# A planner that counts TensorE's instruction pages, and MLP products mixed into the attention from the seventh chunk

## The chip, the cores and the metric

One core of one Trainium2 chip runs the kernel. The metric is device time in microseconds (us) of one launch; lower is better. All times of before are of the same program on the same inputs.

## The reference

Inputs: `q`, `k`, `v` of shape (4 batches, 8 heads, 768 tokens, 64), and an MLP's weights. First a retention layer, then a gated MLP on its output:

```python
gamma = 1.0 - 2.0 ** (-5.0 - np.arange(H))
for t in range(S):
    state = gamma * state + einsum('bhd,bhe->bhde', k[:, :, t], v[:, :, t])
    y[:, :, t] = scale * einsum('bhd,bhde->bhe', q[:, :, t], state)
x = y.transpose(0, 2, 1, 3).reshape(B, S, H * D)           # (4, 768, 512)
gate_pre = sum(conv_w[k] * xp[:, k:k + S, :] for k in range(5))   # xp: x with 4 zero rows ahead
gate = 1 / (1 + exp(-gate_pre))
out = (gate * (x @ w_val)) @ w_out
```

The weights come as 64-bit numbers and are turned into float32 on the chip. The two large products are done as three products each (high by high, high by low, low by high part).

## The kernel before, in words

**Attention.** The 768 tokens of 4 batches are cut into 24 chunks of 128 tokens, numbered g = 0 to 23; chunk g is batch g mod 4 of row g // 4. A chunk is 1 MB of `q`, `k`, `v`, `k` (tile `att`, five buffers, `LB`). GpSimd scales its `v` (`decay`, L236). TensorE computes `scores` (L246), VectorE masks them into `u` (`mask`, L256), then TensorE runs `block_a` (products of `u` with `v`, L284, and the first half of the state, L268) and `block_b` (second half of the state, L268, and the products of the two state snapshots with `q`, L284). ScalarE takes the snapshots (`snap`, L279), VectorE writes the result to `x` (`evac`, L329). All these products are of 64x64 tiles. One such float32 matmul appears twice in the trace: `scores` is 32 matmuls there, a chunk with both halves of the state 128.

**MLP.** It works on a row of four chunks (512 columns of `x`), in 4 tiles m of 128 channels. `split` makes the high and low parts of `x` (L338 on ScalarE, L342 on GpSimd). `conv` is five taps into a PSUM tile `acc`: the first on ScalarE, four on VectorE (L432, "taps" below), of which the planner may give two to TensorE (`pe_tap`, L441). A sigmoid follows (L448). `val_tile` is 12 matmuls of 128x512 (L458), `gated` multiplies by the gate on VectorE (L467), and ScalarE and GpSimd split the result (L474, L478). `out_tile` is 12 matmuls (L486), a copy and a store. There are 24 tiles of each kind, 576 matmuls.

**Weights.** Eight weight tiles `wst` of 512 KB (four buffers) are converted (`convert`): five VectorE instructions (L375, L381, L387, L391, L404), a ScalarE and a GpSimd step in between (L396, L400), then the split (L415, L419). L404 waits for GpSimd's L400.

**PSUM.** The first `EARLY` chunks use two banks of scores in turn (`sy`, and `sy1`, which prints as `sy_97`). From chunk `EARLY` on only `sy` is used; the place of `sy1` goes to the MLP's `mm` tiles, and `block_b` of a chunk ends with the `scores` of the next one.

**The order.** Every step is declared with a due time, an engine, a cost, and what it reads and writes. `plan` (L50) sorts the steps by due time, then runs a list scheduler over them: an engine takes, among its steps that are ready by the declared costs, the one of earliest due time. The order that results is each engine's program; the due times and the costs themselves do nothing on the chip. Each engine runs its instructions strictly in that order and waits where an input is late. The first MLP product may come only after the last user of `sy1`:

```python
if n == m == i == 0:
    steps[-1].after = [
        s for s in steps if any(isinstance(k, Slot) and k.ring in ("s1", "y1") for k in s.reads + s.writes)
    ]
```

Of the kernel before, what the change touches and what calls it, by code (L numbers as in the profile page):

```python
# [18 lines left out]
NPAIR = 4  # L19
TAPS = 5  # L20
WARM = 13
EARLY = 10
LB = 5
XB = 4
XS = 6
GV = 6
LATENCY, LANDING = 0.15, 1.8
TINY = 2.0 ** -15 * (1.0 + 1.0 / 8.0)
LO, HI = slice(0, HALF), slice(HALF, P)

# [8 lines left out]
class Step:  # L39
    def __init__(self, due, engine, cost, reads, writes, fn, args):  # L40
        self.due, self.engine, self.cost, self.fn, self.args = due, engine, cost, fn, args
        self.reads, self.writes = reads, writes
        self.waits, self.then = set(), []
        self.next = []
        self.after = []
        self.ready = 0.0
        self.other = None


def plan(steps):  # L50

    steps = sorted(steps, key=lambda s: s.due)
    writer, readers, rings, users = {}, {}, {}, {}
    for i, s in enumerate(steps):
        s.index = i
        for k in s.writes:
            if isinstance(k, Slot) and k not in users:
                users[k] = []
                rings.setdefault(k.ring, []).append((k, s))
        for k in s.reads + s.writes:  # L60
            if isinstance(k, Slot):
                users[k].append(s)

    def wait(s, b):
        if b is not s and s not in b.then:
            s.waits.add(b.index)
            b.then.append(s)

    for s in steps:
        for k in s.reads + s.writes:  # L70
            if k in writer:
                wait(s, writer[k])
        for k in s.writes:
            for b in readers.pop(k, []):
                wait(s, b)
        for k in s.reads:
            readers.setdefault(k, []).append(s)
        for k in s.writes:
            writer[k] = s
        for b in s.after:  # L80
            wait(s, b)
    for ring in rings.values():
        for i, (k, s) in enumerate(ring):
            if i >= k.bufs:
                for b in users[ring[i - k.bufs][0]]:
                    wait(s, b)
            if i and s not in ring[i - 1][1].next:
                s.waits.add(ring[i - 1][1].index)
                ring[i - 1][1].next.append(s)
    clock, free = {}, {}  # L90

    def offer(s):
        free.setdefault(s.engine, []).append(s)
        if s.other:
            free.setdefault(s.other[0], []).append(s)

    for s in steps:
        clock.setdefault(s.engine, 0.0)
        if not s.waits:
            offer(s)  # L100
    order = []
    while any(free.values()):
        start, _, e = min(
            (max(clock[e], min(s.ready for s in f)), e, e) for e, f in free.items() if f
        )
        s = min((s for s in free[e] if s.ready <= start), key=lambda s: (s.engine != e, s.index))
        free[s.engine].remove(s)
        if s.other:
            free[s.other[0]].remove(s)
            if s.engine != e:  # L110
                s.engine, s.cost, s.fn = s.other
        order.append(s)
        clock[e] = start + s.cost
        for t in s.next:
            t.ready = max(t.ready, start)
            if t not in s.then:
                t.waits.discard(s.index)
                if not t.waits:
                    offer(t)
        for t in s.then:  # L120
            late = LANDING if e == "DMA" else 0.0 if t.engine == e else LATENCY
            t.ready = max(t.ready, clock[e] + late)
            t.waits.discard(s.index)
            if not t.waits:
                offer(t)
    assert len(order) == len(steps)
    return order
# [3 lines left out]
def tile_retention_gated_mlp(  # L131
# [215 lines left out]
    raws = {}  # L347

    def load_w(n):
        st = stage.tile([P, 512, 2], I32, name="wst", bufs=4)  # L350
        nc.sync.dma_start(
            out=st,
            in_=w64[n // 4, n % 4].bitcast(I32).rearrange("p (n two) -> p n two", two=2),
        )
        raws[n] = st

    cvt = {}
# [166 lines left out]
    LATE_AT = 28.7  # L524
    LATE_STEP = 3.05
    MLP_AT = 31.2
    MLP_STEP = 12.8
    SPLIT_LEAD = 5.4
    CONV_LEAD = 6.1
    W_AT = (14.4, 15.6, 15.6, 22.7, 32.7, 35.7, 38.7, 41.7)  # L530

    def load_at(due, g):
        a = [("att", g % LB, "qk"), ("att", g % LB, "vk")]
        if g == 0:
            at(due, "DMA", 1.4, [], a[0:1], load, g, slice(0, 2))
            at(due, "DMA", 0.2, [], ["small"], get, small_sb, small)
            at(due, "DMA", 1.4, [], a[1:2], load, g, slice(2, 4))
            at(due, "DMA", 0.1, [], ["cwraw"], get, cw_raw,
               conv_w.bitcast(I32).rearrange("p (n two) -> p n two", two=2))
            at(due, "DMA", 0.1, [], ["pos"], get, pos_sb, pos)  # L540
        else:
            at(due, "DMA", 2.6, [], a, load, g)
# [14 lines left out]
    def attention(g, t, ahead):  # L557
# [6 lines left out]
        sc = scored[g]  # L564
        y = Slot("y%d" % bank, 1)
        slow = 1.3 if g < 8 else 1.0
        at(t - 3.0, "POOL", 1.05, ["small"], [vk], decay, g)
        if not (g and ahead_of(g - 1)):
            at(t, "PE", 0.6 * slow, [qk, "sy%d" % bank], [sc], scores, g)
            if bank in summed:  # L570
                steps[-1].after.append(summed[bank])
        u = Slot("u", 2)
        at(t + 0.7, "DVE", 0.7, [sc, "small"], [u], mask, g)
        taken = [Slot("snap", 3) for _ in range(2)]
        z = ("z", b)
        if c > 0:
# [1 line left out]
        else:  # L578
            taken = taken[1:]
        at(t + 1.5, "PE", 1.05 * slow, [u, vk], [y, z], block_a, g)  # L580
        at(t + 2.7, "ACT", 0.38, [z], taken[-1:], snap, g, 1)
        more, new = [], []
        if ahead and g + 1 < NG:
            scored[g + 1] = Slot("s%d" % bank, 1)
            more, new = [("att", (g + 1) % LB, "qk")], [scored[g + 1]]
        at(t + 3.3, "PE", (1.5 if ahead else 0.9) * slow, [qk, vk] + taken + more, [y, z] + new,
           block_b, g, ahead)
        summed[bank] = steps[-1]
        if b == 0:
            xbufs[c] = Slot("x", XB)  # L590
            last = [xbufs[c - 1]] + [("x", c - 1, i) for i in range(B)] if c else []
            at(t + 3.5, "ACT" if c else "DVE", 0.25, last,
               [xbufs[c]] + [("x", c, i) for i in range(B)], new_x, c)
        at(t + 5.0, "DVE", 0.7, [y, ("dec", c % 2), xbufs[c]], [("x", c, b)], evac, g)
        if g + LB < NG:
            load_at(t + 3.4, g + LB)
        if c + 1 < NCH:
# [5 lines left out]
    def convert(t, n):  # L603
        raw = wsts[n] if n != "cw" else "cwraw"
        acc, top, rest = Slot("acc", 2), Slot("top", 2), Slot("rest", 2)
        k = 0.25 if n == "cw" else 1.0
        for i, (engine, cost, fn, reads, writes) in enumerate((
            ("DVE", 0.7, cv_bits, [raw], [acc, top, rest]),
            ("DVE", 0.7, cv_top, [raw, acc], [top]),
            ("DVE", 0.7, cv_exp, [top], [acc]),  # L610
            ("DVE", 0.7, cv_rest, [raw, acc], [rest]),
            ("ACT", 0.67, cv_size, [raw], [acc]),
            ("POOL", 1.1, cv_sum, [top], [rest]),
            ("DVE", 0.7, cv_flush, [acc], [rest] if n != "cw" else [rest, "cw"]),
        )):
            at(t + 0.01 * i, engine, cost * k, reads, writes, fn, n)
        if n != "cw":
            at(t + 0.08, "ACT", 0.62, [rest], [("wh", n)], cv_round, n)
            at(t + 0.09, "POOL", 1.3, [rest, ("wh", n)], [("wl", n)], cv_low, n)

    wsts = [Slot("wst", 4) for _ in range(2 * NPAIR)]

    def load_w_at(t, n):
        at(t, "DMA", 1.3, [], [wsts[n]], load_w, n)
# [1 line left out]
    def conv(n, m, t):  # L626
# [1 line left out]
        x = [xbufs[n]] + [("x", n, b) for b in range(B)]  # L628
        at(t, "ACT", 0.7, x + ["cw"], [acc], tap, n, m, 0)
        for k in range(1, TAPS):  # L630
            at(t + 0.1 * k, "DVE", 0.76, x + ["cw", ("diag", m)], [acc], tap, n, m, k)
            if k <= 2:
                steps[-1].other = ("PE", 1.05, pe_tap)
        gates[n, m] = Slot("gate", 2)
# [10 lines left out]
    def val_tile(n, m, t):  # L645
        bank = Slot("mm", 2)
        gate_of = gates[n, m]
        for i in range(3 * NPAIR):
            part = i // NPAIR
            reads = [("wl" if part == 1 else "wh", m)]  # L650
            reads.append(parts[n, i % NPAIR][part == 2])
            at(t + MM * i, "PE", MM, reads, [bank], val, n, m, i)
            if n == m == i == 0:
                steps[-1].after = [
                    s for s in steps if any(isinstance(k, Slot) and k.ring in ("s1", "y1") for k in s.reads + s.writes)
                ]
        gv, gl = gparts[n, m] = Slot("gvh", GV), Slot("gvl", GV)
        at(t + 3.0, "DVE", 0.7, [bank], [gate_of], gated, n, m)
        at(t + 3.1, "ACT", 0.62, [gate_of], [gv], round_gv, n, m)
        at(t + 3.2, "POOL", 1.3, [gate_of, gv], [gl], rest_gv, n, m)  # L660

    def out_tile(n, b, t, cols=1):
        width = DM // cols
        for q in range(cols):
# [3 lines left out]
            for i in range(3 * NPAIR):  # L668
                ct = i // 3
                reads = [gparts[n, ct][i % 3 == 2], ("wl" if i % 3 == 1 else "wh", 4 + ct)]  # L670
                at(t0 + i * MM / cols, "PE", MM / cols, reads, [bank], outp, n, b, i, cs)
            o = Slot("o", 2)
            at(t0 + 12 * MM / cols + 0.1, "ACT", 0.6 / cols, [bank], [o], store, n, b, cs)
            at(t0 + 12 * MM / cols + 0.2, "DMA", 0.1, [o], [], send, n, b, cs)
# [3 lines left out]
    at(0, "ACT", 1.5, [], ["table"], first_sigmoid)  # L678
    load_at(0, 0)
    for due, w, n in ((0.1, 1, 0), (0.2, 0, 1), (0.3, 1, 1), (0.4, 0, 2), (0.5, 1, 2), (0.6, 0, 3), (0.7, 1, 3), (0.8, 0, 4)):  # L680
        (load_w_at if w else load_at)(due, n)
        if due == 0.3:
            at(due, "DMA", 0.2, [], ["eye"], get, eye_sb, eye)
    at(5.05, "PE", 1.0, ["pos", ("att", 0, "vk")], ["sy1"], first_pos)
# [120 lines left out]
```

## Time and profile before

| | us |
|---|---|
| three timed runs | 237.19, 239.09, 240.62; median 239.09 |
| the profiled execution, its own time | 237.6 |
| its span, first to last instruction | 235.8 |
| TensorE busy | 210.0 (89% of the span) |
| VectorE busy | 140.0 (59%) |
| ScalarE, GpSimd busy | 105.4, 105.7 (45% each) |
| mean granted TensorE clock | 0.957 |

The time is the span and 1.8 us around it. Three views matter: the busy time of each engine by stretch, with the granted clock (1.00 is 2.4 GHz, 0.50 is 1.2 GHz); the chain that ended last, which is followed back from the last instruction and names at each step what it waited for ("issue" is a wait for nothing that the profile shows); and the instructions of one engine in order of time.

### The profile page before, as it was taken

What the parts mean: (1) busy time and instruction counts of PE and PEld (TensorE: products, weight loads), DVE (VectorE), ACT (ScalarE), POOL (GpSimd) and SP (SyncE); (2) the same over time, 40 slices, a digit from 0 to 9 for tenths busy, and PEclk for the clock granted to TensorE, in tenths of its full rate; (3) what the DMA queues carried; (4) which work ended last, traced back from release to release, by engine and by line L of the source; (5) the groups of instructions that cost most, each with busy time, mean ns of one, the idle gap of its engine ahead of it and who ended that gap; (6) DMA issues with size and microseconds to landing.
All of it is one profiled execution on the core that took longest, in us unless ns stands there. A gap on an engine that the chain in (4) does not pass through costs nothing.

```text
span 235.8 us, 7969 instructions
## 1 busy us (share of the span) xinstructions
PE 210.0 (89%) x3553; PEld 165.6 (70%) x3553; DVE 140.0 (59%) x211; ACT 105.4 (45%) x218; POOL 105.7 (45%) x93
## 2 busy tenths in 40 slices
PE   8356675767989999999999999999999999999994
PEld 3255574556667777776767788887888888888884
DVE  0575655957878899897435973349816961831100
ACT  2371337427445766650256233664366426520312
POOL 0274549764984996131138112492168208220400
PEclk9977559979999999999999999999999999999999
DMA  5999949997835665655010111111111111111122
GB/s 169 384 425 417 403 140 383 327 327 267 327 113 197 226 199 200 210 231 211 10 40 3 47 47 46 46 46 44 47 44 44 44 44 47 57 64 56 44 92 89
DMA packets 8822, 36.32 MB, mean 154 GB/s; under 512 B 1106, under 2 KB 1618, under 8 KB 5844
## 3 DMA queue, kind: packets, MB, share of 16 engines
q1 hardware_dynamic: 8788, 35.82, 40.7%
q8 instruction: 28, 0.46, 0.8%
q14 instruction: 6, 0.05, 0.1%
HBM read 29.52 MB, written 6.29 MB: 152 GB/s over the span
## 4 chain that ended last, share of the span: by engine, by line
PE 83%; issue 7%; DMA 6%; DVE 1%; ACT 1%; SPq 0%; ACTq 0%
PE mm L458 30%; PE mm L486 29%; PE sy L284 11%; DMA att<-in_att_dram 6%; PE sy L246 6%; PE z_ps L268 6%; PE acc L441 1%; DVE x L329 1%; DVE u L256 1%; ACT snap L279 0%; ACT dec L317 0%; ACT acc L430 0%; ACT o_sb L496 0%; SPq L224 0%; ACTq L496 0%
## 5 line engine op out<-in xcount | busy, mean ns | idle before, releaser
L432 DVE SCALAR_TENSOR_TENSOR acc<-x,cw_sb,acc 128x512 f32<-128x512 f32 x93 | 69.4, 753 | 21.1 <-ACT acc L430 18.9
L478 POOL TENSOR_TENSOR gvl<-gate,gvh 128x512 fp32r<-128x512 f32 x24 | 30.9, 1297 | 38.9 <-ACT gvh L474 29.3
L342 POOL TENSOR_TENSOR xl<-x,xh 128x512 fp32r<-128x512 f32 x24 | 30.5, 1291 | 30.7 <-PE mm L458 30.7
L236 POOL TENSOR_TENSOR att<-att,small_sb 128x512 f32<-128x512 f32 x24 | 25.0, 1044 | 32.2 <-DMA att<-in_att_dram 23.8
L486 PE MATMUL mm<-woh,gvl 128*128 128x512 f32 (+1 forms) x100 | 39.0, 390 | 0.0
L486 PE MATMUL mm<-wol,gvh 128*128 128x512 f32 (+1 forms) x100 | 39.0, 390 | 0.0
L486 PE MATMUL mm<-woh,gvh 128*128 128x512 f32 (+1 forms) x100 | 38.9, 389 | 0.0
L496 ACT COPY o_sb<-mm 128x512 f32<-128x512 f32 (+1 forms) x25 | 14.3, 571 | 37.3 <-PE mm L486 37.3
L279 ACT COPY snap<-z_ps 128x256 f32<-128x256 f32 x44 | 15.0, 374 | 33.4 <-PE z_ps L268 31.8
L467 DVE TENSOR_TENSOR gate<-mm,gate 128x512 f32<-128x512 f32 x24 | 16.5, 689 | 20.6 <-PE mm L458 20.5
L458 PE MATMUL mm<-xh,wvh 128*128 128x512 f32 x96 | 28.5, 408 | 0.0
L256 DVE TENSOR_TENSOR u<-sy,small_sb 128x512 f32<-128x512 f32 x24 | 16.5, 688 | 17.9 <-PE sy L246 17.9
L458 PE MATMUL mm<-xh,wvl 128*128 128x512 f32 x96 | 27.1, 402 | 0.0
L458 PE MATMUL mm<-xl,wvh 128*128 128x512 f32 x96 | 26.8, 397 | 0.0
L246 PE MATMUL sy<-att 64*64 64x64 f32 x768 | 20.7, 240 | 6.4 <-issue 5.8
L268 PE MATMUL z_ps<-att 64*64 64x64 f32 x704 | 22.5, 242 | 2.8 <-issue 2.7
L284 PE MATMUL sy<-att,snap 64*64 64x64 f32 x704 | 18.5, 232 | 6.9 <-issue 6.9
L268 PEld LDWEIGHTS z_ps<-att 64*64 64x64 f32 x704 | 17.7, 152 | 8.4 <-ACT snap L279 4.4
L474 ACT CAST gvh<-gate 128x512 fp32r<-128x512 f32 x24 | 14.9, 621 | 19.4 <-DVE gate L467 13.7
L284 PEld LDWEIGHTS sy<-u,att 64*64 64x64 f32 x768 | 16.2, 150 | 10.3 <-issue 7.7
L246 PEld LDWEIGHTS sy<-att 64*64 64x64 f32 x768 | 17.5, 153 | 8.2 <-issue 6.8
L284 PE MATMUL sy<-u,att 64*64 64x64 f32 x768 | 19.3, 240 | 4.0 <-issue 2.3
(46 smaller groups left out, 270.7 us busy)
## 6 DMA issues: line engine op xcount, KB each, us to landing
att<-in_att_dram SPq DMA_DIRECT2D x23, 1024.0 KB, 7.0
out_dram<-o_sb SPq DMA_DIRECT2D x23, 256.0 KB, 2.0
wst<-in_w_dram SPq DMA_DIRECT2D x8, 512.0 KB, 8.7
att<-in_att_dram SPq DMA_DIRECT2D x2, 512.0 KB, 5.2
out_dram<-o_sb SPq DMA_DIRECT2D x2, 128.0 KB, 1.7
small_sb<-in_small_dram SPq DMA_DIRECT2D x1, 68.0 KB, 4.0
eye_sb<-in_eye_dram SPq DMA_DIRECT2D x1, 64.0 KB, 8.0
cw_raw<-in_conv_w_dram SPq DMA_DIRECT2D x1, 20.0 KB, 5.8
```

Of the source, the lines that this page charges most:

```text
L236: nc.gpsimd.tensor_tensor(v, v, vd_sb[:, c, :].unsqueeze(2).broadcast_to([P, 8, HALF]), op=ALU.mult)
L246: nc.tensor.matmul(sy[cols, x, (2 * j + s) * HALF:(2 * j + s + 1) * HALF], lhsT=kT[rows, x, j, s, :], rhs=q[rows, x, j, s, :], start=True, ...
L256: nc.vector.tensor_tensor(us[g], sy[:, :, 0:256].rearrange("p x (a t) -> p x a t", t=HALF), tri_sb.unsqueeze(1).unsqueeze(1).broadcast_to( ...
L268: nc.tensor.matmul(z_ps[cols, x, b, j], lhsT=k[rows, x, j, s, :], rhs=v[rows, x, j, s, :], start=g == 0 and s == 0 and j == 0, stop=True, ...
L279: nc.scalar.copy(sn, z_ps[:, :, b])
L284: nc.tensor.matmul(sy_of(g)[cols, h, off:off + HALF], lhsT=lhsT, rhs=rhs, start=start, stop=True, skip_group_check=True,)
L342: nc.gpsimd.tensor_tensor(xl[n, ct], xs[n][:, ct, :, HALO:], xh[n, ct].bitcast(F32), op=ALU.subtract)
L432: nc.vector.scalar_tensor_tensor(acc, x[:, :, k:k + P], cw_sb[:, m, k:k + 1], acc, op0=ALU.mult, op1=ALU.add,)
L458: nc.tensor.matmul(vps[n, m], lhsT=w[:, m, ct * P:(ct + 1) * P], rhs=xx[n, ct].rearrange("p b t -> p (b t)"), start=(i == 0), stop=(i == 3 ...
L467: nc.vector.tensor_tensor(gv, vps.pop((n, m)), gv, op=ALU.mult)
L478: nc.gpsimd.tensor_tensor(gvl, gate.pop((n, m)), gvh.bitcast(F32), op=ALU.subtract)
L486: nc.tensor.matmul(ops[n, b, cs.start][:, 0:cs.stop - cs.start], lhsT=gg[:, b * P:(b + 1) * P], rhs=w[:, ct, cs], start=(i == 0), stop=(i ...
```

## The change

- `EARLY` goes from 10 to 6: chunks 0 to 5 use two score banks, and MLP products may stand from chunk 6 on.
- `MLP_STEP` goes from 12.8 to 10.2 and the first weight's due time from 14.4 to 9.3, so that MLP steps and the first conversion have an earlier due time.
- The declared costs of VectorE's steps go from 0.70 to 0.62 and from 0.76 to 0.68.
- `plan` counts the words of TensorE's program: each step on TensorE gets a number of words, and when a page of 128 is used up, TensorE's clock in the plan is held to at least 4.0 us after the page before.
- `decay` gets a due time that is never ahead of that of its chunk's load. The load of the eighth weight comes ahead of that of chunk 11. The four weight buffers and five chunk buffers stay as they were.

```diff
-EARLY = 10
+EARLY = 6
 LB = 5
+WB = 4
...
+PAGE, FETCH = 128, 4.0
...
-    order = []
+    order, words, paged = [], PAGE - 28, [0.0, 0.0]
...
         clock[e] = start + s.cost
+        if e == "PE" and s.words:
+
+            left, now = s.words, start
+            while left >= words:
+                now += s.cost * words / s.words
+                left -= words
+                paged.append(now)
+                now, words = max(now, paged[-2] + FETCH), PAGE
+            words -= left
+            clock[e] = max(clock[e], now + s.cost * left / s.words)
...
-    MLP_STEP = 12.8
+    MLP_STEP = 10.2
...
-    W_AT = (14.4, 15.6, 15.6, 22.7, 32.7, 35.7, 38.7, 41.7)
+    W_AT = (9.3, 15.6, 15.6, 22.7, 32.7, 35.7, 38.7, 41.7)
...
-        at(t - 3.0, "POOL", 1.05, ["small"], [vk], decay, g)
+        at(max(t - 3.0, loaded[g] + 0.01), "POOL", 1.05, ["small"], [vk], decay, g)
...
-        at(t + 0.7, "DVE", 0.7, [sc, "small"], [u], mask, g)
+        at(t + 0.7, "DVE", 0.62, [sc, "small"], [u], mask, g)
...
+        steps[-1].words = 96 if ahead else 64
...
-            at(t + 0.1 * k, "DVE", 0.76, x + ["cw", ("diag", m)], [acc], tap, n, m, k)
+            at(t + 0.1 * k, "DVE", 0.68, x + ["cw", ("diag", m)], [acc], tap, n, m, k)
```

TensorE's program is the same up to the end of chunk 5. What follows there (`sy_97<-att,snap` is the end of chunk 5's `block_b`, `mm` an MLP product, `acc<-x,diag` a `pe_tap`), before:

```order
L268 MATMUL z_ps<-att 64x64 x8
L284 MATMUL sy_97<-att,snap 64x64 x16
L246 MATMUL sy_97<-att 64x64 x16
L284 MATMUL sy<-u,att 64x64 x16
L268 MATMUL z_ps<-att 64x64 x8
L441 MATMUL acc<-x,diag 128x512
L268 MATMUL z_ps<-att 64x64 x8
L284 MATMUL sy<-att,snap 64x64 x16
L284 MATMUL sy_97<-u,att 64x64 x16
```

and now:

```order
L281 MATMUL z_ps<-att 64x64 x8
L297 MATMUL sy_97<-att,snap 64x64 x16
L297 MATMUL sy<-u,att 64x64 x16
L281 MATMUL z_ps<-att 64x64 x8
L469 MATMUL mm<-xh,wvh 128x512 x4
L281 MATMUL z_ps<-att 64x64 x8
L297 MATMUL sy<-att,snap 64x64 x16
L259 MATMUL sy<-att 64x64 x16
L469 MATMUL mm<-xh,wvl 128x512 x4
L469 MATMUL mm<-xl,wvh 128x512 x4
L469 MATMUL mm<-xh,wvh 128x512 x2
L297 MATMUL sy<-u,att 64x64 x16
```

The scores of chunk 7 went behind chunk 6's `block_b`, the `pe_tap` is gone, and 4 and then 10 MLP matmuls stand where attention followed attention.

VectorE's program from the mask of chunk 7 to that of chunk 8 (`u` is a mask, `x` an evacuation, `acc<-x` a tap, `gate` a `gated`, the rest conversion of weights), before:

```order
L256 TENSOR_TENSOR u<-sy_97,small_sb 128x512
L404 SCALAR_TENSOR_TENSOR rest<-acc,rest 128x512
L375 TENSOR_SCALAR acc<-wst 128x512
L432 SCALAR_TENSOR_TENSOR acc<-x,cw_sb,acc 128x512
L329 TENSOR_TENSOR x<-sy,dec 128x4x128
L432 SCALAR_TENSOR_TENSOR acc<-x,cw_sb,acc 128x512
L381 SCALAR_TENSOR_TENSOR top<-wst,acc 128x512
L256 TENSOR_TENSOR u<-sy,small_sb 128x512
```

and now:

```order
L269 TENSOR_TENSOR u<-sy,small_sb 128x512
L415 SCALAR_TENSOR_TENSOR rest<-acc,rest 128x512
L342 TENSOR_TENSOR x<-sy,dec 128x4x128
L478 TENSOR_TENSOR gate<-mm,gate 128x512
L443 SCALAR_TENSOR_TENSOR acc<-x,cw_sb,acc 128x512
L386 TENSOR_SCALAR acc<-wst 128x512
L392 SCALAR_TENSOR_TENSOR top<-wst,acc 128x512
L398 TENSOR_SCALAR acc<-top 128x512
L402 SCALAR_TENSOR_TENSOR rest<-wst,acc 128x512
L386 TENSOR_SCALAR acc<-wst 128x512
L392 SCALAR_TENSOR_TENSOR top<-wst,acc 128x512
L269 TENSOR_TENSOR u<-sy,small_sb 128x512
```

Between the two masks stand ten instructions in place of six. Over the whole program the two kernels have the same attention and MLP matmuls; of `pe_tap` there are three before and one now, and VectorE has two taps more.

## Rows read from the trace of the kernel before

**Rows 1.** The page: TensorE and VectorE in 40 slices of 5.9 us, tenths busy
```profile
PE   8356675767989999999999999999999999999994
DVE  0575655957878899897435973349816961831100
```
**Rows 2.** By stretch: length; PE, PEld, DVE, ACT, POOL busy (instructions); PE clock, DMA share, GB/s
```profile
15.60:40.60 25.00, 14.94 (x539) 13.53 (x543) 14.38 (x23) 10.28 (x25) 15.42 (x14) 0.73 0.88 341
40.60:61.50 20.90, 15.48 (x663) 12.64 (x654) 15.03 (x23) 9.40 (x23) 14.00 (x13) 0.92 0.85 305
61.50:82.00 20.50, 19.81 (x456) 15.14 (x457) 17.36 (x27) 11.22 (x25) 16.13 (x15) 1.00 0.57 205
82.00:110.00 28.00, 27.60 (x697) 21.12 (x687) 25.27 (x38) 15.34 (x34) 14.66 (x13) 1.00 0.58 206
```
**Rows 3.** By stretch, cut where TensorE stops in the trace; columns as in rows 2
```profile
37.55:40.31 2.76, 0.00 (x0) 0.00 (x0) 1.17 (x2) 2.15 (x4) 2.76 (x3) 1.00 1.00 399
40.31:43.62 3.31, 3.31 (x127) 2.33 (x127) 2.19 (x4) 0.94 (x3) 1.95 (x2) 1.00 0.87 291
43.62:46.53 2.91, 2.32 (x128) 2.04 (x127) 2.84 (x5) 1.09 (x3) 2.51 (x3) 1.00 0.99 394
46.53:48.91 2.38, 0.00 (x1) 0.00 (x0) 1.36 (x3) 0.47 (x2) 2.31 (x3) 0.92 0.91 322
48.91:52.62 3.71, 3.70 (x127) 3.40 (x127) 1.81 (x3) 0.86 (x4) 2.18 (x2) 0.59 0.89 318
```
**Rows 4.** The chain that ended last, in order of time: start us, us, what
```profile
41.35 0.41 PE sy L284 x28
...
42.05 1.06 PE acc L441 x2
...
61.56 2.29 PE mm L458 x9
63.85 0.62 PE sy L284 x32
...
70.91 0.62 PE sy L284 x32
...
87.52 0.62 PE sy L284 x32
...
93.58 0.62 PE sy L284 x32
...
94.44 0.90 PE mm L458 x3
...
96.66 2.05 PE mm L458 x8
98.72 0.62 PE sy L284 x32
...
133.03 0.62 PE sy L284 x32
...
137.46 2.80 PE mm L458 x12
...
232.76 0.37 ACT o_sb L496
```
**Rows 5.** VectorE in order of time: start us, us, operation [idle before, releaser]
```profile
37.37 0.69 DVE L256 TENSOR_TENSOR u<-sy,small_sb 128x512 f32<-128x512 f32 x1
...
41.40 0.69 DVE L329 TENSOR_TENSOR x<-sy,dec 128x512 f32<-128x512 f32 x1 [2.68 <-PE sy L246]
```
**Rows 6.** VectorE alone, one stretch: length, busy (instructions), PE clock, DMA share, GB/s
```profile
41.00:94.00 53.00, 44.22 (x68) 0.97 0.68 242
```
**Rows 7.** Waits, 41 to 94 us: who for whom, us in total, times, longest
```profile
DVE rest L404 <- POOL rest L400: 1.2, 1, 1.2
```
**Rows 8.** The page: DMA issues, KB each, median us from issue to landing
```profile
att<-in_att_dram SPq DMA_DIRECT2D x23, 1024.0 KB, 7.0
...
wst<-in_w_dram SPq DMA_DIRECT2D x8, 512.0 KB, 8.7
```

More of the change, by code (lines that the diff above doesn't have):

```diff
@@ L46, in __init__ @@
         self.ready = 0.0
+        self.words = 0
         self.other = None
@@ L349, in load_w @@
     def load_w(n):
[L350 to L354, printed above, removed]
+        st = stage.tile([P, 512, 2], I32, name="wst", bufs=WB)
+        src = w64[n // 4, n % 4].bitcast(I32).rearrange("p (n two) -> p n two", two=2)
+        nc.sync.dma_start(out=st, in_=src)
         raws[n] = st
@@ L526, in tile_retention_gated_mlp @@
     MLP_AT = 31.2
-    MLP_STEP = 12.8
+    MLP_STEP = 10.2
     SPLIT_LEAD = 5.4
     CONV_LEAD = 6.1
-    W_AT = (14.4, 15.6, 15.6, 22.7, 32.7, 35.7, 38.7, 41.7)
+    W_AT = (9.3, 15.6, 15.6, 22.7, 32.7, 35.7, 38.7, 41.7)
+    loaded = {}
     def load_at(due, g):
+        loaded[g] = due
         a = [("att", g % LB, "qk"), ("att", g % LB, "vk")]
@@ L566, in attention @@
         slow = 1.3 if g < 8 else 1.0
-        at(t - 3.0, "POOL", 1.05, ["small"], [vk], decay, g)
+        at(max(t - 3.0, loaded[g] + 0.01), "POOL", 1.05, ["small"], [vk], decay, g)
         if not (g and ahead_of(g - 1)):
             at(t, "PE", 0.6 * slow, [qk, "sy%d" % bank], [sc], scores, g)
+            steps[-1].words = 32
             if bank in summed:
@@ L580, in attention @@
         at(t + 1.5, "PE", 1.05 * slow, [u, vk], [y, z], block_a, g)
+        steps[-1].words = 64
         at(t + 2.7, "ACT", 0.38, [z], taken[-1:], snap, g, 1)
@@ L593, in attention @@
                [xbufs[c]] + [("x", c, i) for i in range(B)], new_x, c)
-        at(t + 5.0, "DVE", 0.7, [y, ("dec", c % 2), xbufs[c]], [("x", c, b)], evac, g)
+        at(t + 5.0, "DVE", 0.62, [y, ("dec", c % 2), xbufs[c]], [("x", c, b)], evac, g)
         if g + LB < NG:
@@ L607, in convert @@
         for i, (engine, cost, fn, reads, writes) in enumerate((
[L608 to L611, printed above, removed]
+            ("DVE", 0.62, cv_bits, [raw], [acc, top, rest]),
+            ("DVE", 0.62, cv_top, [raw, acc], [top]),
+            ("DVE", 0.62, cv_exp, [top], [acc]),
+            ("DVE", 0.62, cv_rest, [raw, acc], [rest]),
             ("ACT", 0.67, cv_size, [raw], [acc]),
             ("POOL", 1.1, cv_sum, [top], [rest]),
-            ("DVE", 0.7, cv_flush, [acc], [rest] if n != "cw" else [rest, "cw"]),
+            ("DVE", 0.62, cv_flush, [acc], [rest] if n != "cw" else [rest, "cw"]),
         )):
@@ L619, in convert @@
             at(t + 0.09, "POOL", 1.3, [rest, ("wh", n)], [("wl", n)], cv_low, n)
-    wsts = [Slot("wst", 4) for _ in range(2 * NPAIR)]
+    wsts = [Slot("wst", WB) for _ in range(2 * NPAIR)]
     def load_w_at(t, n):
@@ L652, in val_tile @@
             at(t + MM * i, "PE", MM, reads, [bank], val, n, m, i)
+            steps[-1].words = 1
             if n == m == i == 0:
@@ L657, in val_tile @@
         gv, gl = gparts[n, m] = Slot("gvh", GV), Slot("gvl", GV)
-        at(t + 3.0, "DVE", 0.7, [bank], [gate_of], gated, n, m)
+        at(t + 3.0, "DVE", 0.62, [bank], [gate_of], gated, n, m)
         at(t + 3.1, "ACT", 0.62, [gate_of], [gv], round_gv, n, m)
@@ L671, in out_tile @@
                 at(t0 + i * MM / cols, "PE", MM / cols, reads, [bank], outp, n, b, i, cs)
+                steps[-1].words = 1
             o = Slot("o", 2)
@@ L680, in tile_retention_gated_mlp @@
     for due, w, n in ((0.1, 1, 0), (0.2, 0, 1), (0.3, 1, 1), (0.4, 0, 2), (0.5, 1, 2), (0.6, 0, 3), (0.7, 1, 3), (0.8, 0, 4)):
-        (load_w_at if w else load_at)(due, n)
+        if w or n < LB:
+            (load_w_at if w else load_at)(due, n)
         if due == 0.3:
```

## The prediction

> **What bounds the kernel now.** I read the engines' rows in slices first: TensorE is at 9 tenths from the eleventh slice to the end, so whatever is saved must come from the first 60 us [rows 1]. The table by stretch, read next, gives the size: from 40.60 to 61.50 TensorE is busy for 15.48 of 20.90 us, 5.4 idle; from 61.50 to 110 it idles 0.69 and 0.40 [rows 2]. From 137.46 on the chain is MLP products alone, 12 in 2.80 us, or 0.233 each, without a wait [rows 4]. So TensorE's work sets the end, and a us of idleness taken out early is a us off the time, if nothing takes its place.
>
> Cutting the early stretch where TensorE stops shows what the idleness is [rows 3]. Between two stops it runs 127 or 128 matmuls, each with a weight load, that is 256 instructions; the stops do not care which step they fall in. They cost 2.76 and 2.38 us here, with DMA at 0.91 to 1.00 busy. Behind the second one the granted clock falls to 0.59, a mixture of 1.2 and 2.4 GHz, and the next 128 matmuls take 3.71 us. I read the stops as TensorE waiting for its next block of instructions. Small matmuls use a block up in about 3 us, while a chunk with 11 MLP products takes 5.14 us (93.58 to 98.72, [rows 4]), and the stops of two us are gone there.
>
> The Trainium skill speaks against this ("Runtime: NRT & Kernel Launch", section "Instruction fetch mechanics"): instructions come in blocks of 256, TensorE holds 2048 of them, and crossing a block is mostly hidden. The trace agrees on 256 and not on hidden (2.76 and 2.38 us). If the page is right, the stops have another cause and need not go away; that is the second rival.
>
> **The change part by part.** Chunks 0 to 5: TensorE's order is the same, VectorE gets up to three conversion steps more ahead of a mask. It is busy for 14.38 of 25.0 us there [rows 2] and TensorE stands at its own stops; I take 0. If that cover fails, three steps cost 3 x 0.65 = 2.0 us; a gain has no source there.
>
> Start of the mixing. Chunk 6's `block_a` stands at about 41.3 before [rows 4]; the 0.5 us of scores ahead of it move back, so it comes at 40.8, just behind the stop that ends at 40.31 [rows 3]. Its mask was done by 38.1 [rows 5]; with four taps now ahead of it VectorE gets to it some 2 us later, still in time.
>
> TensorE's need. A mixed chunk of 5.14 us holds 11 products (3 and 8, [rows 4]): 5.14 - 11 x 0.233 = 2.57 us for the attention part. 87.52 to 93.58 with 15 products gives 2.56. In the new order chunks 6 to 14 hold 106 products (58 before, in chunks 10 to 14) and one `pe_tap` of 1.06 us [rows 4]: 9 x 2.57 + 106 x 0.233 + 1.06 = 48.9 us. By TensorE alone `block_a` of chunk 15 would start at 89.7; it starts at 87.52 before. Those 48 more products are worth 11.2 us, so break-even is 98.7.
>
> VectorE's need. This is what takes the idleness's place. From chunk 5's evacuation, which cannot start before chunk 5 ends (41.40, [rows 5]), to the mask of chunk 15 the new order has 77 instructions; all of 41 to 94 us held 68 [rows 6]. A VectorE instruction takes 44.22 / 68 = 0.650 us there, and 25.27 / 38 = 0.665 in the stretch with many taps [rows 2]. The new stretch is of that kind: 77 x 0.665 = 51.2. The mask then starts at 92.6 and ends at 93.3, behind TensorE's 89.7. VectorE was planned at 0.62 and 0.68, so the order gives it no slack. Waits on others come on top: the nearest row is one wait of 1.2 us for GpSimd's conversion step [rows 7]. Bounds are 0 and that wait once per chunk, 9 x 1.2 = 10.8; I take it once, as the row has it: 94.5.
>
> GpSimd and the queues. The decays move ahead in GpSimd's queue, where conversion sums and splits stand behind them. A chunk's load lands 7.0 us after its issue, a weight's after 8.7 [rows 8], while `plan` counts 2.6 + 1.8 = 4.4 and 3.1, so a decay can hold GpSimd. With chunks of about 5.9 us the sums are still ready by the masks that follow: 0 in the sum, up to the 10.8 above in the range. The eighth weight's load now goes ahead of chunk 11's on SyncE's queue: that chunk is used five chunks later, some 27 us against 7.0, so 0, or at worst one weight's transfer.
>
> From chunk 15 to 23: 45.5 us before (87.52 to 133.03, [rows 4]) with 99 products; now 79, so 45.5 - 20 x 0.233 = 40.8, the short issue waits of that stretch kept as they are. VectorE has few instructions there. Behind chunk 23: 232.76 - 133.03 = 99.7 before with 431 products, 28 fewer now: 93.2.
>
> Sum: 94.5 + 40.8 + 93.2 = 228.5 against 232.76, a gain of 4.3 us. On the profiled execution's own 237.6 (span 235.8 and 1.8 around it) that is 233.3. That execution lies 1.5 below the median of the runs, 239.09; from the median it would be 234.8. I take 234.0 between them.
>
> **The rivals.**
> *VectorE does not bind* (0.20): it overlaps its instructions better than 0.665, or its lateness falls where TensorE has products left. Then 89.7 + 40.8 + 93.2 = 223.7, a gain of 9.1: 228.5. For it: VectorE's instructions have run at 0.650 on average in that time. Against it: it needs 48.9 / 77 = 0.635 with no wait at all, and a tap heavy stretch has never had that.
>
> *The stops come back, or queues give all back* (0.20): with MLP products in between, a stop still comes after each 256 instructions. The stretch's idleness of 5.4 us stays, the gain of 4.3 is gone, and the time is 237.6 to 239. Against it: in 82 to 110 us TensorE runs 697 matmuls, more than five blocks, and idles 0.40 us [rows 2]. For it: 63.85 to 70.91 took 7.06 us for a chunk with 15 products, 1 us above 2.57 + 15 x 0.233 = 6.07, so some of it can stay.
>
> *GpSimd holds VectorE* (0.10), the slower side: place, chunks 6 to 14; a decay waits for its load, the conversion sum behind it is late, VectorE's L404 ahead of the next mask waits for it, and TensorE for the mask. Price: 1.2 us in each of nine chunks, 93.3 + 10.8 = 104.1, which is 5.4 behind break-even: 243. It decides once these nine chunks take over 6.4 us each on average (98.7 - 40.8 over nine), and is measurable from about 7.0. Against it: 5.9 is what I expect, and loads are asked for five chunks ahead.
>
> **How the numbers follow.** The forecast has 0.50, the rivals 0.20, 0.20 and 0.10. A measurement of this kernel can tell about 2% from no change, some 4.8 us; my forecast lies near that bound, so its chance is halved between faster (0.25) and within 2% (0.25). With the first rival faster has 0.45, with the second and a tenth of the last the middle has 0.46, slower keeps 0.09. The range reaches from the first rival's 228.5 to the second's 239; outside lie the last rival and about half of the first.
>
> **What would show it.** Right: no stop over 1 us in TensorE behind 45 us; a chunk of 5.5 to 6.2 us between 41 and 94; VectorE at 0.9 or more of that stretch, and TensorE's largest waits there before L297's products with `u`, released by VectorE; `block_a` of chunk 15 at 93 to 96 us; the dense tail of products starting at 138 to 142 us with 28 products fewer behind chunk 23. Wrong: chunk 15 at 91 or earlier (VectorE never bound), stops of 2 us that go on after each 128 matmuls (they are not what mixing hides), or waits of VectorE for GpSimd of over 5 us in total.

## The result and the profile after

| | before | after |
|---|---|---|
| median of 20 runs, us | 237.82 (236.17 to 240.90) | 235.52 (234.50 to 240.74) |
| the profiled execution, us | 237.6 | 235.24 |
| its span, us | 235.8 | 233.5 |

The ratio is 0.9915, 95% interval 0.9886 to 0.9944: faster, by some 0.85%, which is within the 2%. The forecast was 234.0 (228.5 to 239.0). For one program below, that of the runs e8 and e9, I compare medians of all runs, since the ratio given for e9, 0.9687, counts only its runs of 229.85 and 231.33 and leaves out four that lie over 1.5% above the lowest.

The page of the changed kernel, in slices of 5.8 us, and two of its lines of totals:

```profile
PE 209.3 (90%) x3549; PEld 163.5 (70%) x3549; DVE 140.2 (60%) x213; ACT 105.7 (45%) x218; POOL 105.7 (45%) x93
...
PE   8276666998799998897998999999999999999994
...
DVE  0488678999999998322296636169617861921100
...
PEclk9975697999999999998899999999999999999999
...
q8 instruction: 28, 0.46, 0.8%
```

Against [rows 1], TensorE's row has new dents at the 16th, 17th and 19th slice (88 to 99 and 105 to 111 us), and VectorE is at 9 tenths or near it from the 8th slice to the 16th. The last line is used in the experiments: 3549 matmuls and 3549 weight loads are 7098 instructions, or 27.7 blocks of 256, and 28 instruction packets of 16 KB were fetched.

The changed kernel by stretch, columns as in [rows 2]:

```profile
15.60:40.60 25.00, 16.20 (x595) 14.35 (x594) 20.27 (x33) 13.38 (x32) 20.25 (x18) 0.74 0.93 362
40.60:61.50 20.90, 19.32 (x453) 14.63 (x457) 20.52 (x32) 12.45 (x28) 16.03 (x15) 0.98 0.67 255
61.50:82.00 20.50, 19.52 (x541) 14.80 (x533) 20.06 (x31) 13.72 (x30) 14.36 (x14) 1.00 0.58 207
82.00:95.00 13.00, 12.10 (x317) 9.13 (x319) 10.90 (x17) 4.32 (x11) 5.54 (x5) 1.00 0.59 209
95.00:110.00 15.00, 12.26 (x338) 9.33 (x331) 3.03 (x6) 5.39 (x14) 5.58 (x5) 0.99 0.54 186
110.00:140.00 30.00, 29.25 (x732) 21.98 (x731) 18.14 (x28) 11.52 (x25) 9.71 (x8) 0.95 0.21 78
```

From 40.60 to 61.50 TensorE now idles 1.58 us (5.42 before, [rows 2]): the change did what it says. But from 82 to 110 it idles 0.90 + 2.74 = 3.64, against 0.40 [rows 2]. Most of the idleness moved by 50 us.

What the two profiled executions differ by stands ahead of chunk 6. The start of its `block_a` in TensorE's order, before and now:

```profile
41.08 0.26 PE L284 MATMUL sy<-u,att 64*64 64x64 f32 x2
38.71 0.31 PE L297 MATMUL sy<-u,att 64*64 64x64 f32 x1
```

From there to the last copy, at 232.76 before [rows 4] and at 230.40 now, it is 191.7 us in both.

The chain that ended last, in order of time, columns as in [rows 4]:

```profile
38.21 0.94 PE sy L297 x16
...
92.72 0.69 PE sy L297 x32
...
95.41 0.39 PE sy L259 x25
95.80 0.90 issue
96.69 0.34 PE sy L259 x7
...
101.93 0.26 issue
102.18 0.56 PE sy L259 x19
...
107.43 1.51 issue
108.93 0.68 PE sy L259 x29
...
137.20 0.62 PE sy L297 x32
...
140.70 2.80 PE mm L469 x12
...
230.40 0.37 ACT o_sb L507
```

Chunk 15's `block_a` stands at 92.72, chunk 23's at 137.20, the dense tail begins at 140.70. Between them are three waits for "issue", each in the middle of `scores`: behind 25, 13 and 3 of the 32. Cut there, as in [rows 3]:

```profile
95.80:96.69 0.89, 0.00 (x0) 0.00 (x0) 0.00 (x0) 0.00 (x0) 0.48 (x1) 1.00 0.61 74
96.69:101.92 5.23, 5.23 (x127) 3.94 (x128) 1.29 (x2) 2.67 (x8) 1.04 (x1) 1.00 0.47 191
102.18:107.43 5.25, 5.17 (x128) 3.82 (x127) 1.29 (x2) 2.72 (x6) 1.19 (x1) 1.00 0.69 253
107.43:108.93 1.50, 0.00 (x0) 0.00 (x0) 0.00 (x0) 0.00 (x0) 1.50 (x3) 1.00 0.38 44
108.93:112.00 3.07, 3.07 (x38) 2.06 (x42) 1.89 (x3) 0.47 (x1) 2.08 (x2) 0.63 0.78 320
```

It is the picture of [rows 3] again: 127 or 128 matmuls between two stops. The three stops are 0.90 + 0.26 + 1.51 = 2.67 us; behind the longest the granted clock is 0.63 for 3.07 us, which by this row costs an estimated 3.07 x (1 - 0.63) = 1.1 more.

### The profile page after: what moved, and what is told of

It is laid out like the page before. It is cut to its first block, busy times and chain, and to the rows that moved or that the text cites. A ratio compares the mean times of both kernels' runs of the same rounds, so it can differ in the third digit from the quotient of the medians.

```text
span 233.5 us, 7952 instructions
## 1 busy us (share of the span) xinstructions
PE 209.3 (90%) x3549; PEld 163.5 (70%) x3549; DVE 140.2 (60%) x213; ACT 105.7 (45%) x218; POOL 105.7 (45%) x93
## 4 chain that ended last, share of the span: by engine, by line
PE 61%; DVE 19%; issue 7%; POOL 5%; ACT 3%; DMA 3%; SPq 0%; POOLq 0%; ACTq 0%; DVEq 0%
PE mm L497 27%; PE mm L469 22%; DVE acc L443 9%; PE sy L297 6%; PE sy L259 3%; DMA att<-in_att_dram 3%; PE z_ps L281 3%; DVE x L342 3%; DVE u L269 2%; POOL rest L411 2%; POOL att L249 2%; DVE gate L478 1%; ACT xh L351 1%; DVE rest L415 1%; POOL wvl L430 1%
## 5 line engine op out<-in xcount | busy, mean ns | idle before, releaser
L443 DVE SCALAR_TENSOR_TENSOR acc<-x,cw_sb,acc 128x512 f32<-128x512 f32 x95 | 70.5, 753 | 17.2 <-ACT acc L441 15.1
L355 POOL TENSOR_TENSOR xl<-x,xh 128x512 fp32r<-128x512 f32 x24 | 30.5, 1284 | 31.8 <-PE mm L469 28.5
L497 PE MATMUL mm<-woh,gvh 128*128 128x512 f32 (+1 forms) x100 | 39.4, 394 | 0.0
L249 POOL TENSOR_TENSOR att<-att,small_sb 128x512 f32<-128x512 f32 x24 | 25.1, 1044 | 29.1 <-DMA att<-in_att_dram 27.3
L469 PE MATMUL mm<-xl,wvh 128*128 128x512 f32 x96 | 28.5, 407 | 0.0
L469 PE MATMUL mm<-xh,wvl 128*128 128x512 f32 x96 | 28.1, 404 | 0.0
L297 PEld LDWEIGHTS sy<-u,att 64*64 64x64 f32 x768 | 16.0, 152 | 14.4 <-issue 5.8
L259 PE MATMUL sy<-att 64*64 64x64 f32 x768 | 18.8, 232 | 7.4 <-issue 6.3
L292 ACT COPY snap<-z_ps 128x256 f32<-128x256 f32 x44 | 14.5, 371 | 19.0 <-PE z_ps L281 19.0
L259 PEld LDWEIGHTS sy<-att 64*64 64x64 f32 x768 | 15.9, 147 | 9.0 <-issue 7.0
L497 PEld LDWEIGHTS mm<-woh,gvh 128*128 128x128 f32 x100 | 18.9, 189 | 4.2
```

Of the source, the lines that this page charges most:

```text
L249: nc.gpsimd.tensor_tensor(v, v, vd_sb[:, c, :].unsqueeze(2).broadcast_to([P, 8, HALF]), op=ALU.mult)
L259: nc.tensor.matmul(sy[cols, x, (2 * j + s) * HALF:(2 * j + s + 1) * HALF], lhsT=kT[rows, x, j, s, :], rhs=q[rows, x, j, s, :], start=True, ...
L297: nc.tensor.matmul(sy_of(g)[cols, h, off:off + HALF], lhsT=lhsT, rhs=rhs, start=start, stop=True, skip_group_check=True,)
L355: nc.gpsimd.tensor_tensor(xl[n, ct], xs[n][:, ct, :, HALO:], xh[n, ct].bitcast(F32), op=ALU.subtract)
L443: nc.vector.scalar_tensor_tensor(acc, x[:, :, k:k + P], cw_sb[:, m, k:k + 1], acc, op0=ALU.mult, op1=ALU.add,)
L469: nc.tensor.matmul(vps[n, m], lhsT=w[:, m, ct * P:(ct + 1) * P], rhs=xx[n, ct].rearrange("p b t -> p (b t)"), start=(i == 0), stop=(i == 3 ...
```

## The experiments

Chunk times below go from `block_a` to `block_a`, read from TensorE's instructions in order of time. "Own need" is the prediction's formula, 2.57 us a chunk, 0.233 a product and 1.06 for a `pe_tap`.

**e1, thin taps, and e5, a thin VectorE.** Does VectorE set the pace of chunks 6 to 14? The order is that of the changed kernel; e1 lets most taps run on 16 of 128 tokens, e5 also converts only 64 columns of the last four weights.

```diff
+            wide = 16 if n <= 2 else P
...
-                acc, x[:, :, k:k + P], cw_sb[:, m, k:k + 1], acc,
+                acc[:, :, 0:wide], x[:, :, k:k + wide], cw_sb[:, m, k:k + 1], acc[:, :, 0:wide],
```

> The changed kernel with VectorE's taps 1 to 4 of the first three rows cut to 16 of each 128 tokens; every engine's order is the same. VectorE binds chunks 6 to 14: with about 35 taps of 0.75 us made short there, block_a of chunk 15, at 92.7 us in the changed kernel, starts at 90 or before, and VectorE's busy share of 41 to 92 falls below 0.75. Rival, something else sets the pace of these chunks (instruction blocks, GpSimd): chunk 15 stays within 1 us of 92.7.

> The thin taps of the first experiment and, beside them, VectorE's five instructions on each of the weights 4 to 7 cut to 64 of 512 columns (the conversion sum on GpSimd keeps its length but works on other data); every engine's order is the same. VectorE's conversions and evacuations hold chunks 6 to 8: chunk 6 to 9 falls from 20.2 us to 17.5 to 18.5 (need of TensorE 17.1), and chunk 15 starts at 88.5 to 90.5. Rival, the slow clock behind the stop before chunk 6 and the late blocks hold them: 19.5 us or more, and chunk 15 at 91 or later.

Measured: 233.90 and 233.85 us, one run each. By stretch, e1:

```profile
40.60:61.50 20.90, 20.02 (x445) 15.28 (x447) 17.02 (x32) 11.71 (x27) 15.06 (x13) 0.92 0.68 257
61.50:82.00 20.50, 19.50 (x549) 14.84 (x540) 12.66 (x32) 13.87 (x31) 15.55 (x14) 1.00 0.58 204
```

and e5:

```profile
38.50:61.50 23.00, 23.00 (x567) 18.07 (x564) 10.95 (x34) 12.14 (x28) 16.05 (x16) 0.89 0.70 254
61.50:82.00 20.50, 18.59 (x473) 13.79 (x472) 12.20 (x32) 14.01 (x31) 15.51 (x15) 1.00 0.58 210
```

VectorE's 20.06 us from 61.5 to 82 fall to 12.66 and 12.20, but chunk 15 starts at 91.8 and 91.4, against 92.7: 0.9 and 1.3 us for at least 15 us less work (51.5 us in the changed kernel from 40.6 to 95, 35.8 in e1). Chunk 6 was longer in these two runs (8.6 and 8.1 us against 7.3, at a lower clock), so I also count from chunk 7: 46.7 us to chunk 15 in the changed kernel, 45.0 and 44.9 here, own need 43.1. VectorE holds up to 1.8 us of the 3.6 above the own need. Chunk 6 to 9 took 19.3 us in e5 (20.2 in the changed kernel), between the two expectations.

The chain says where these chunks are bound. Its shares by line, first in the changed kernel (61.5 to 92.8 us), then in e1 (61.5 to 92 us; L355 is a `split`, L249 a `decay`):

```profile
by line: DVE acc L443 60.3%; issue 8.5%; DVE x L342 8.5%; DVE gate L478 8.4%; DVE u L269 7.9%; POOL rest L411 4.2%; DVE rest L415 2.2%; ACT gate L459 1.9%; ACT acc L441 1.9%; PE sy L297 0.8%; ACTq L459 0.1%
by line: PE mm L498 20.9%; PE mm L470 20.3%; POOL xl L355 13.8%; PE sy L297 12.9%; PE z_ps L281 7.4%; POOL att L249 6.6%; PE sy L259 6.1%; issue 4.8%; POOL gvl L490 4.3%; POOL wol L430 4.1%
```

So VectorE does bind them in the changed kernel, but TensorE and GpSimd stand 1 to 2 us behind it: it is a bound that little hangs on.

**e2, the program moved by 36 matmuls.** Four large warm-up matmuls go, forty small ones come, all ahead of chunk 0. If stops belong to blocks of TensorE's program, they come 36 matmuls earlier in the attention; if they belong to a step or a wait for data, they stay at their step.

```diff
-WARM = 13
+WARM = 9
...
+    at(0, "PE", 0.0, [], ["sy1"], warm_small, 0)
+    at(0, "PE", 0.0, [], ["sy1"], warm_small, 1)
```

> The changed kernel with 4 of its 13 warm-up matmuls replaced by 40 small ones (36 matmuls more at the start), everything behind in the same order. The stops are blocks of 256 instructions that come late: the stops in chunks 15 to 17, which fall in the scores of the next chunk after 25, 13 and 3 of 32 matmuls, move 36 matmuls ahead in the order, into the products with the snapshots or the second state half; between two stops stand 127 or 128 matmuls as before. Rival, they are waits that belong to the scores (a load, a buffer): they stay inside the scores.

Measured: 236.97 us, one run. TensorE in order of time (start, us, operation, count, idle before and what ended it):

```profile
94.61 0.69 PE L297 MATMUL sy<-u,att 64*64 64x64 f32 x32
96.64 0.53 PE L297 MATMUL sy<-att,snap 64*64 64x64 f32 x21
99.32 0.58 PE L297 MATMUL sy<-att,snap 64*64 64x64 f32 x10 [2.15 <-issue]
```

In the changed kernel the stop of chunk 15 stood behind 25 of 32 `scores`. Here it stands in the snapshot products just ahead of them, with 11 of those left (10 in this row, and one more): 25 + 11 is 36 matmuls earlier, as many as were put in. Counted from the start of the program, the same 2135 matmuls stand ahead of both stops, first the changed kernel, then e2 (columns: length, PE busy and matmuls, clock, DMA share, GB/s):

```profile
0.00:96.60 96.60, 78.23 (x2135) 0.91 0.73 271
0.00:97.50 97.50, 79.32 (x2135) 0.89 0.71 268
```

So the stops belong to blocks of 128 matmuls with their loads. Which blocks stop is another matter: this stop is longer, 2.15 against 0.90, the two in chunks 16 and 17 are gone, and two new ones end at 80.59 and 85.97 (1.08 and 0.36), 128 matmuls apart.

**e3, no late loads.** The loads of chunks 17 to 23 are left out, so that DMA is quiet behind chunk 15.

```diff
+        if g >= 17:
+            tiles[g] = tiles[g - LB]
+            return
```

> The changed kernel in which chunks 17 to 23 are not loaded; they compute on the data that stands in the buffer of five chunks before. The order of all engines but SyncE is the same. If the blocks come late in chunks 15 to 18 because the loads of 1 MB keep the DMA engines busy, the stops of 0.90, 0.26 and 1.51 us between 95 and 109 us vanish, chunk 15 to 23 takes 41 to 42 us in place of 44.5, and the time falls by 2 to 3 us against the changed kernel (235.5). Rival, a block takes over 5 us in any case: the stops stay, and the time is within 1 us of 235.5.

Measured: 233.09 us median, ratio 0.9811 (0.9715 to 0.9906). TensorE in order of time:

```profile
92.23 0.69 PE L300 MATMUL sy<-u,att 64*64 64x64 f32 x32 [0.67 <-DVE x L345]
...
95.56 0.34 PE L262 MATMUL sy<-att 64*64 64x64 f32 x7 [0.26 <-issue]
...
101.05 0.56 PE L262 MATMUL sy<-att 64*64 64x64 f32 x19 [0.25 <-issue]
...
106.70 0.69 PE L262 MATMUL sy<-att 64*64 64x64 f32 x29 [0.42 <-issue]
...
112.44 0.28 PE L300 MATMUL sy<-att,snap 64*64 64x64 f32 x3 [0.91 <-issue]
```

and by stretch, chunk 15 to 23:

```profile
92.20:134.80 42.60, 39.80 (x1059) 30.03 (x1059) 21.21 (x32) 16.07 (x38) 12.80 (x11) 1.00 0.06 22
```

With DMA at 0.06 the stops stay at the same matmuls (0.26, 0.25, 0.42 against 0.90, 0.26, 1.51), with a fourth of 0.91 in chunk 18, and the clock does not fall: chunk 15 to 23 takes 42.6 in place of 44.5. The four come to 1.84 us, where the changed kernel has 2.67 in one execution and, in e10, 3.00 (0.63, 0.52, 0.95 and 0.90 at the same four places). So the loads lengthen the arrival of a block and with it the stops, by about a third, but stops are left without them: the rival was right on the stops, the theory on the time. In the changed kernel a block's instruction packet starts at 94.2, 99.7 and 106.5, some 2.4 us ahead of the end of each stop (96.69, 102.18, 108.93). From entering a block to the packet for the next one it was 3.0 and 4.4 us; in e3 2.8, 3.0 and 3.1. The packet at 106.5 in the DMA view, cut to 106 to 107 us:

```profile
q8 instruction: 1, 0.02, 6.1%
```

**e4, no page counting.** `PAGE, FETCH = 128, 0.0`, all else as changed.

> The changed kernel with the planner's wait for a page set from 4.0 us to 0, so that it plans without pages, all else kept. If counting the pages is what brings the gain, this is no faster than before (237.8) or slower. If the gain is that of mixing from chunk 6, with VectorE as the bound, it stands at the changed kernel's 235.5 within 1 us. As the order here gives chunks 15 to 22 some 11 products each instead of 5 to 11, it may also be 1 to 2 us faster, if few products per chunk bring the late stops.

Measured: 237.90 us median, ratio 0.9993 (0.9945 to 1.0042): the gain is gone. Without the count the plan puts 19 products into chunk 8 and 1 into chunk 9, and TensorE then waits for VectorE's evacuation, as its instructions in order of time show:

```profile
68.66 1.13 PE L297 MATMUL sy<-u,att 64*64 64x64 f32 x32 [3.24 <-DVE x L342]
```

This run also tests whether more products per chunk end the late stops, and they do not: chunks 15 to 22 hold 91 products here, 10 to 13 each, and still have four stops (0.64, 0.50, 0.96 and 1.34 us). They took 46.2 us, 4.4 above the own need. The longest:

```profile
121.39 0.40 PE L297 MATMUL sy<-att,snap 64*64 64x64 f32 x11 [1.34 <-issue]
```

**e6, early mixing alone, and e7, all but that.** e6 is the kernel before with `EARLY = 6`; e7 is the changed kernel with `EARLY = 10`.

> The kernel before with EARLY at 6 and nothing else: mixing from the seventh chunk, planned with the old costs and without pages. If mixing alone is the gain: 235 to 236 us. If the planner's page counting is needed for it, as the fourth experiment says: 237 to 239.5, no faster than before.

> The changed kernel with EARLY back at 10: pages counted and new costs, but products mixed in from the eleventh chunk only. If mixing is needed for the gain: 237 to 240 us. If the gain is in the first six chunks (chunk 6 starts 2.4 us earlier in the changed kernel, TensorE's order there being the same) it stays: 235 to 236.5.

Measured: e6 236.22 us median, ratio 0.9887 (0.9813 to 0.9961); e7 241.13, ratio 1.011 (1.0039 to 1.0180). Mixing from chunk 6 gives the whole gain by itself; the new costs, due times and pages without it lose 1.1%. With e4 this says that the page count is needed only beside the new costs and due times; the old plan does as well without it. In e6 TensorE still stops behind chunk 15, for 1.47 and 1.46 us, with 93 products in chunks 15 to 22 (45.9 us, 3.7 above the own need), so the old plan has the same fault there.

**e8 and e9, the real words.** The plan's count is wrong twice: it counts 160 words for a chunk (32, 64 and 96 or 64), where the trace has 128 matmuls, and it gives a page 4.0 us, where the blocks that begin at 96.69, 102.18 and 108.93 are 5.5 and 6.8 us apart. e8 sets both right, and the tap's cost to the 0.755 us it takes; e9 is the same program run again, beside the next three.

```diff
-PAGE, FETCH = 128, 4.0
+PAGE, FETCH = 128, 5.3
...
-        steps[-1].words = 64
+        steps[-1].words = 48
...
-        steps[-1].words = 96 if ahead else 64
+        steps[-1].words = 80 if ahead else 48
```

> The changed kernel planned with what its trace shows: 48 words for block_a and 80 for block_b with scores (32, 16 and 32 matmuls each), 5.3 us from one block to the next, 0.755 us for a tap. Chunks 15 to 22 then hold 10 to 12 products each (89 in all, 79 before this edit), and 390 are left behind chunk 23 in place of 403. If late blocks in chunks with few products cost the changed kernel its gain, chunk 15 to 23 loses 1 to 2 us less and the time is 233 to 234.5. If the stops depend on where in a block the products stand, and not on how many there are: 235 to 236.5, as the changed kernel.

> The kernel of the run with the real words a second time, beside the changed kernel and on the same base. Theory (TensorE is paced by its program's pages, and the planner's counts of it were too low): 0.978 to 0.987 of the kernel before, and at least 0.4% below the changed kernel; chunk 15 to chunk 23 in 43 to 44 us. Rival (both plans are equal and the 0.9817 of the first run was the spread of three rounds): 0.988 to 0.994, the same as the changed kernel.

> The changed kernel itself, as the mark for the other three. Both theories: 0.989 to 0.994 of the kernel before, with chunk 15 to chunk 23 in 44 to 45 us and a stop of about 1.5 us in the scores of chunk 17.

Measured: e8 234.88 us median, between its two expectations, ratio 0.9817 (0.9727 to 0.9906); e9 233.86, 229.85 to 239.04 over six runs; e10 235.73, ratio 0.9900 (0.9854 to 0.9946), 234.15 to 237.15 over six. Chunk 15 to 23 now holds 89 products in place of 79, own need 8 x 2.57 + 89 x 0.233 = 41.3 us; it took 43.5 (e8) and 42.2 (e9), 2.2 and 0.9 above it. The changed kernel has an own need of 39.0 there and took 44.5, and 43.7 in e10: 5.5 and 4.7 above. TensorE's matmuls show no wait for "issue" of over 0.2 us behind 45 us in e8 and e9. So this plan removes most of what the changed kernel gave back there. Why it does is open. It is not the number of products alone, since e4 and e6 have more and stop. One difference in the traces: in e8 and e9 two instruction packets start within the block that ends some 5 us ahead of chunk 15 and holds 16 products; in the changed kernel that block has one packet and 12 products. First the changed kernel, 81.1 to 86.6 us, then e8, 85.5 to 91.7 us:

```profile
q8 instruction: 1, 0.02, 1.0%
q8 instruction: 2, 0.03, 3.6%
```

No run tests whether this lead is the cause.

At chunk 6, though, the profiles of e8 and e9 differ, with one program. The same stop, ahead of the last 26 `scores`, and what stands behind it, first e8:

```profile
42.62:44.86 2.24, 0.00 (x1) 0.00 (x1) 1.67 (x3) 0.17 (x1) 1.91 (x2) 0.91 0.94 366
44.86:49.76 4.90, 4.90 (x35) 4.01 (x36) 1.93 (x4) 0.62 (x1) 2.32 (x2) 0.50 0.85 344
```

then e9:

```profile
41.01:42.43 1.42, 0.00 (x2) 0.00 (x1) 1.35 (x3) 0.39 (x1) 1.42 (x2) 1.00 0.94 392
42.43:45.79 3.36, 3.36 (x38) 2.52 (x38) 3.02 (x5) 0.62 (x1) 1.54 (x2) 1.00 1.03 417
```

With 2.24 us of stop the clock goes to 0.50 (1.2 GHz) for 4.9 us and chunk 6 takes 11.3 us; with 1.42 it stays at 1.00 and chunk 6 takes 7.8. That is 3.5 of the 5.4 us between the two profiled executions (235.29 and 229.85). The changed kernel shows the same: chunk 6 took 7.3 us in the first profile and 9.6 in e10, which has a stop of 1.66 within it. Over all runs the medians are 234.25 (10 runs of this program), 235.62 (26 of the changed kernel) and 237.82 (57 of the one before). This version is probably the fastest, but with runs of e9 and e10 that overlap, the step of 1.4 us from the changed kernel is not sure.

**e11, two rates, and e12, old costs.** Both start from e8. e11 gives a page 6.0 us until the plan's 36 us, to put more products into chunk 6; e12 sets VectorE's costs back to 0.70, but for the tap.

```diff
-                now, words = max(now, paged[-2] + FETCH), PAGE
+                now, words = max(now, paged[-2] + (6.0 if now < 36 else 5.3)), PAGE
```

> As the run with the real words, but a page is given 6.0 us until the plan's 36 us and 5.3 us behind them, so that more products go into chunk 6 and fewer small matmuls stand in a row there. Theory (the stop of 2.24 us at chunk 6 and the 4.9 us at a clock of 0.50 behind it cost 2 to 4 us, and they hang on the block's arrival): chunk 6 to 7 falls from 11.3 us to 6.5 to 8.5 us and the time to 231 to 234 us, 0.970 to 0.982 of the kernel before. Rival (the stop moves to another chunk, with the clock behind it): 234 to 236 us, the same as the run with the real words.

> As the run with the real words, but the planner's new VectorE costs are set back to the 0.7 us of the kernel before, except the tap's. Theory (VectorE's declared costs matter little, since the run with thin taps moved chunk 15 by 0.9 us only): within 0.5% of the run with the real words, 0.978 to 0.988 of the kernel before. Rival (VectorE's true costs are what places the products rightly): 0.99 to 1.00, with VectorE waits of over 1 us before evacuations in chunks 6 to 14.

Measured: e11 236.67 us median, ratio 0.9930 (0.9890 to 0.9969); e12 235.70, ratio 0.9883 (0.9834 to 0.9932). e11 is nearer to its rival, and slower than both expectations: the stop ahead of 26 `scores` at chunk 6 is there again (1.89 us, ending at 44.75), the clock behind it too (0.72 from 46 to 50), and chunk 6 took 10.3 us. The plan did not come out as I wanted it: chunk 6 holds 12 products, 15 in e8. Whether that stop can be planned away stays open. e12 lies between the two expectations: no wait of VectorE over 0.84 us, but no better than the changed kernel. What VectorE's declared costs are worth stays open.

## Why the prediction came out as it did

| step | predicted | measured |
|---|---|---|
| `block_a` of chunk 6 | 40.8 | 38.7 |
| chunk 6 to chunk 15 | 53.7 | 54.0 |
| chunk 15 to chunk 23 | 40.8 | 44.5 |
| chunk 23 to the last store | 93.2 | 93.2 |
| start of the last copy | 228.5 | 230.4 |

**The stops are instruction blocks: right, and now shown**, by e2, by the 28 packets and by their starts, some 2.4 us ahead of the end of each stop. The Trainium skill ("Runtime: NRT & Kernel Launch", section "Instruction fetch mechanics") calls the crossing of a block mostly hidden; the runs agree with its 256 instructions, and not with hidden where TensorE stops: 2.24 us in e8, and still 0.25 to 0.91 with the loads gone. The second rival's premise, that a stop comes after each 256 instructions whatever stands between, was right as to where; but most blocks of the mixed chunks pass without one.

**Chunk 6's start: early by 2.1 us, and in the profiled pair this is the whole gain.** The prediction had "a gain has no source there". The stop ahead of it took 1.37 us (it ends at 38.21), where the trace of before had 2.76 [rows 3], in the same TensorE program. From chunk 6 on nothing was gained: 7.6 us more up to chunk 15, 1.1 less to chunk 23, 6.5 less behind it. Whether the change brought the early start is open. The six traces with this order start chunk 6 at 37.8 to 38.7, e6 at 38.0, and the two with `EARLY = 10` at 41.1 (before) and 40.2 (e7), which speaks for it; but e8 and e9, one program, differ by 1.6. So that the time fell within the range is in part luck: a term put at 0 made up for what the mixing did not bring.

**Chunk 6 to 15: the sum right, its reason half right.** VectorE runs as predicted, 77 instructions, 0.656 us each (0.665 assumed), 97% busy. Its row of the changed kernel, 41 to 93 us:

```profile
41.00:93.00 52.00, 50.50 (x77) 1.00 0.62 226
```

and TensorE's waits for it there, from the table of waits (us in total, times, longest):

```profile
PE sy L297 <- DVE x L342: 2.9, 4, 0.9
```

It binds, by these waits and by the chain. But e1 and e5 take three tenths or more of its work away and win 0.4 and 1.0 us of the 54.0: with the slow clock of chunk 6 and with GpSimd in the chain, the rest comes to 53.0 to 53.6, and not to TensorE's 48.9. My step "VectorE's need ... takes the idleness's place" named the right engine and had the distance wrong: it put VectorE 4.8 us behind TensorE (94.5 against 89.7), and taking its work away was worth 1 to 2.

**GpSimd and the queues: right at 0.** The waits of VectorE for GpSimd that the third rival needs are absent from that table. TensorE's weight loads do wait 2.5 us in all for a decay (L249), in two waits: small, and outside the sum.

**Chunk 15 to 23: the step that failed.** I had "the short issue waits of that stretch kept as they are" and took 20 products off at 0.233. That was the mis-sized term: 3.7 us. With 99 products, 45.5 us against an own need of 43.6, the excess was 1.9; with 79 the own need falls to 39.0 and the excess grows to 5.5. The stops (2.67) and the slow clock behind them (1.1) are 3.8 of it, and e8 and e9, with 89 products, get it back to 2.2 and 0.9. So the issue waits of that stretch were not kept as they were: part of the first rival's or my own gain returned as the second rival's stops, 50 us later. That they came because products had been taken out is argued and not shown: e4 and e6, with 91 and 93 products, are still 4.4 and 3.7 above the own need.

The sum of the four differences, -2.1 + 0.3 + 3.7 + 0.0, is the 1.9 us by which the end missed 228.5. The gain of 4.3 became 2.4. Of the signs named beforehand, VectorE's share, TensorE's waits for it and the dense tail at 140.70 came true; "no stop over 1 us" did not (1.51), and chunk 15 at 92.7 lies just ahead of the 93 to 96, by the early start alone.

## What to carry to other kernels

Where an engine stops after a constant count of instructions, whatever the step, count the instructions, and do not take it for granted that waits stay as they are in a stretch that you take work out of. Plan with the count and the pace that the trace shows (128 matmuls, some 5.3 us). An engine at 97% is a suspect, and the chain can show that it is last, but not by how much: thin its work with the order kept, and see whether the others move. Cut both traces at the first place where TensorE's two programs differ: a gain that stands ahead of it needs another explanation than the work behind it.

## What the runs showed of the hardware that I had not expected

- A block's arrival is elastic: ahead of the stops of chunks 15 to 18, from entering one block to the packet of the next took 2.8 to 3.1 us with DMA at 0.06 (e3), and up to 4.4 us beside a chunk's load (changed kernel, 102 to 107 us).
- The same stop in the same program can be 1.42 us and leave the granted clock at 1.00, or 2.24 us and be followed by 4.9 us at 0.50; one such event was worth 3.5 us, more than the whole change. The changed kernel has its own, behind 1.37 us at 38.21 (0.57 from 38 to 42 us), so the length of the stop alone does not decide it.
